# Another order of a step's stages and another set of streamed weight halves, in a four-layer attention kernel on one core

## The chip, the cores and the metric

The kernel runs on one core of one Trainium2 chip. The core has a matrix engine (PE, with its weight loads shown as PEld), a vector engine (DVE), a scalar engine (ACT), a general engine (POOL), and a queue engine (SP) that here only issues transfers; 16 DMA engines move data between the chip's memory (HBM) and the core's own memory. Each engine runs its instructions in its own order and waits on semaphores for the others. The metric is the device time of one execution in microseconds (us); lower is better.

## The reference

Two kinds of layer alternate, A, B, A, B, on a sequence of 2048 tokens of width 640. Each is added to its input after a layer norm.

```python
def _A_ref(x, mem0, Wq, Wk, Wv, Wo, seg_len):     # 32 heads of 192, 8 memory tokens, segments of 32
    for s in range(n_seg):                        # 64 segments, one after the other
        h = jnp.concatenate([mem, xs], axis=1)    # 8 + 32 tokens
        ...                                       # q, k, v; masked softmax; p v
        o = jnp.einsum('bhte,hed->btd', o, Wo)
        mem = o[:, :M, :].copy()                  # the next segment's memory
        outs.append(o[:, M:, :])

def _B_ref(x, wqkv, wo):                          # 32 heads of 20; each token sees itself and
    ...                                           # the 7 tokens at distances 2, 4, ... 14 before it

x = x + _A_ref(_layernorm(x), ...)
x = x + _B_ref(_layernorm(x), ...)
x = x + _A_ref(_layernorm(x), ...)                # the same weights again
x = x + _B_ref(_layernorm(x), ...)
```

The segments of an A layer form a chain, because each takes its memory from the one before. A segment has only 40 rows, while the weights of an A layer are 640 x 6144 four times: every segment needs all of them.

## The kernel before

**A step.** The kernel runs 67 steps (0 to 66), written out in full. Step s works on segment s of the first A layer and segment s - 2 of the second A layer at once: both use the same weights, so their rows stand side by side (`l` = 0 and 1, 2 x 40 columns) in every matmul. The B layers run one step behind, on what the step before left (`xr`). The last step has no A work left, and the first no B work.

**Stages.** A step is a list of named stages, `ORDER` (L58 to L63). `stages()` turns it into a list, and the loop in `run` (L585 to L595) calls one function for each word. For the A layers:

- `q0` to `q15`: queries and keys of two heads, 30 matmuls from two weight halves into one accumulator (`qk_ps`, L323, L328); in all but q0 the first half is read by the first 15 matmuls, the second by the last 15. ACT copies the result to one of five `QK` tiles (L330).
- `s0` to `s3`: scores of four such units (eight heads), 32 small matmuls (L340, L346), then the softmax on DVE and ACT (L350 to L363).
- `t0` to `t3`: transposes of the probabilities (L370), and two masked copies on DVE (L373).
- `va`, `vb`, `vc` 0 to 3: values. `va` and `vb` (`v_seg`) read two weight halves each for the segment's rows (L385). `vc` (`v_mem`) reads the same four halves again for the memory rows (L398). ACT copies both to the tile `V` (L389, L402).
- `pv0` to `pv3`: probabilities times values (L411), copied by ACT to `ot` (L414).
- `o0` to `o14`: output projection, one half of Wo each (o14: two), all into one accumulator (L428).

For the B layers: `ln10` (layer norm sums, L298, L299, then DVE and ACT up to `xnB`, L312), `qkv0` (75 matmuls, L473; three ACT copies, L475; then products on DVE and POOL, L480), `logits0` (L489, softmax up to `attn`, L508), `e0` to `e4` (one matmul each, L515, then a product and a sum on DVE, L518, L520, up to `oT`), `wo0` (L527), `ln20` (the norm for the next step's second A segment) and `store0` (every fourth step). `input0` normalises the next 128 input rows (every fourth step), and `alpha0` is one POOL copy (L287) of the next step's input segment.

**What sets the order.** PE and SP run exactly in the order of the list (`manual_schedule`). DVE, ACT and POOL are ordered by the tile framework's scheduler. All waits are set by the framework: a tile's buffer is given to a new tile when the last reader of the old one is done. PE's results share six accumulator buffers; the output projection has its own.

**Weights.** The four A weights are cut into 64 halves of 128 x 1920 bf16 (480 KB): 0 to 31 are keys and queries (2i and 2i + 1 belong to q_i), 32 to 47 values (four for each of the groups 0 to 3), 48 to 63 the output projection. 32 of them (`RESIDENT`) are loaded once and stay. The other 32 (`STREAMED`, L79) are loaded again in every step into the ring `wt`, which has `RING` = 5 buffers. `half(h)` (L236) issues the load at the place of the stage that reads it first: from the weights in step 0 (with a copy to `Wr`, in the order the ring wants), and after that from `Wr` in two transfers of 240 KB each on SP's queue (L250). SP runs ahead of PE until the ring is full; then it stands until PE is done with a half.

Of the kernel before, what the change touches and what calls it, by code (L numbers as in the profile page):

```python
# [55 lines left out]


ORDER = """  # L58
q0 q1 ln10 alpha0 q2 input0 q3 s0 va0 vb0 vc0 qkv0 q4 t0 q5 q6 q7
s1 pv0 va1 vb1 vc1 logits0 q8 o0 q9 t1 o1 e0 q10 o2 e1 o3 q11  # L60
s2 pv1 va2 vb2 vc2 e2 q12 o4 q13 e3 t2 q14 o5 e4 q15 wo0
s3 pv2 va3 vb3 vc3 o6 o7 ln20 store0 t3 o8 o9 pv3 o10 o11 o12 o13 o14
"""  # L63


# [10 lines left out]
PLAN = stages()  # L76


STREAMED = (1, 5, 6, 7, 8, 11, 13, 14, 15, 17, 22, 23, 25, 26, 29, 30, 31, 33, 35, 38, 41, 46, 48, 49, 50, 51, 53, 55, 56, 58, 60, 63)  # L79
RESIDENT = set(range(N_HALVES)) - set(STREAMED)  # L80
assert len(RESIDENT) == N_RESIDENT

# [570 lines left out]
```

## Time and profile before

| what | value |
|---|---|
| median of three runs | 3643.86 us (3640.27 to 3645.96) |
| the profiled execution's own time | 3648.06 us |
| its span on the core | 3646.3 us |
| mean granted clock of PE | 0.982 of full |
| PE, weight loads busy | 90%, 78% of the span |
| DVE, ACT, POOL busy | 55%, 57%, 10% |
| read from HBM | 1059.73 MB, 296 GB/s over the span |
| first q0 to first q0 of step 1 | 124 us |
| a step between step 4 and step 63 | 53.3 us in the mean (51.6 to 56.6) |

A busy share says how long an engine had work, not whether it held the others up. PE has the most, so what counts is the time in which PE stands; the view of waits lists it by who ended it. The chain of waits follows the end of the run back from each piece of work to what released it. "L328" is a line of the kernel; "wt<-Wr" is the load of a streamed half. [...]

### The profile page before, as it was taken

The page shows a single profiled execution, that of the slowest core. Times are in us where ns is not written, and L with a number is a line of the kernel's source. Part 1 is how long each engine was busy: PE and PEld are TensorE (multiplying, and loading weights), DVE is VectorE, ACT ScalarE, POOL GpSimd, SP SyncE. Part 2 cuts the span into 40 slices and gives each one's busy share as a digit, 9 for nine tenths or more (in the row PEclk, how much of TensorE's full clock was granted, in tenths as well). Part 3 has the DMA queues.
Part 4 walks back from the last instruction along what each step waited for, and adds up shares of the span by engine and source line. Part 5 has one row for each costly group of instructions (what it writes and reads, how often), then busy time and mean ns, then how long its engine had stood idle before and what let it go on. Part 6 is the DMA issues. An engine that isn't in the chain of part 4 may idle for free.

```text
span 3646.3 us, 185054 instructions
## 1 busy us (share of the span) xinstructions
PE 3293.8 (90%) x83325; PEld 2826.4 (78%) x83325; DVE 1994.9 (55%) x5057; ACT 2084.7 (57%) x4533; POOL 378.9 (10%) x467
## 2 busy tenths in 40 slices
PE   5789999999999999999999999999999989999997
PEld 3677787787878777777878777887778777778876
DVE  1346556555555655555565555556555555555554
ACT  2355665565655566565556556565666555655554
POOL 3110010110111001011100101110010110111000
PEclk7799999999999999999999999999999999999998
DMA  9989999898989999999999999999999988999995
GB/s 353 343 283 297 298 301 300 294 304 294 304 291 306 297 302 302 298 304 301 295 302 298 299 299 303 297 307 304 303 302 304 300 288 289 303 299 303 301 301 188
DMA packets 646218, 1090.19 MB, mean 299 GB/s; under 512 B 68648, under 2 KB 642736, under 8 KB 645424
## 3 DMA queue, kind: packets, MB, share of 16 engines
q1 hardware_dynamic: 640560, 1060.00, 88.4%
q8 instruction: 651, 10.67, 1.2%
q0 software_dynamic: 2560, 15.73, 1.1%
q10 hardware_dynamic: 2304, 2.62, 0.2%
q14 instruction: 143, 1.17, 0.1%
HBM read 1059.73 MB, written 18.35 MB: 296 GB/s over the span
## 4 chain that ended last, share of the span: by engine, by line
PE 56%; DMA 16%; DVE 11%; ACT 10%; issue 4%; SPq 3%; POOL 0%; ACTq 0%; POOLq 0%; DVEq 0%
PE qk_ps L328 18%; DMA wt<-Wr 12%; PE v_ps L385 9%; PE acc L428 8%; PE v_ps L398 5%; ACT V L389 3%; PE qkv_ps L473 3%; ACT V L402 3%; ACT QK L330 3%; PE s_ps L346 2%; PE o_ps L411 2%; DVE oT L520 2%; PE qk_ps L323 2%; PE s_ps L340 2%; SPq L250 2%
## 5 line engine op out<-in xcount | busy, mean ns | idle before, releaser
L330 ACT CAST QK<-qk_ps 128x480 bf16<-128x480 f32 x1056 | 578.6, 559 | 949.0 <-PE qk_ps L328 699.0
L328 PE MATMUL qk_ps<-ST,wt 128*128 128x80 bf16 x15840 | 718.8, 203 | 62.6 <-DMA wt<-Wr 45.1
L328 PEld LDWEIGHTS <-wt 128*128 128x128 bf16 x15840 | 628.4, 100 | 96.8 <-DMA wt<-Wr 64.9
L328 PE MATMUL qk_ps<-ST,res 128*128 128x80 bf16 x13860 | 625.4, 203 | 11.6 <-issue 6.0
L328 PEld LDWEIGHTS <-res 128*128 128x128 bf16 x13860 | 562.4, 101 | 39.8 <-issue 10.4
L389 ACT CAST V<-v_ps 64x384 bf16<-64x384 f32 x1056 | 495.8, 469 | 150.5 <-PE v_ps L385 131.4
L428 PE MATMUL acc<-ot,wt 128*128 128x80 bf16 x9900 | 498.4, 202 | 17.6 <-DMA wt<-in_A_Wo_dram 8.5
L402 ACT CAST V<-v_ps 32x384 bf16<-32x384 f32 x1056 | 494.7, 468 | 22.5 <-PE v_ps L398 3.2
L385 PE MATMUL v_ps<-res,ST 128*64 128x384 bf16 x3630 | 488.6, 331 | 13.0 <-DMA res<-in_A_Wv_dram 12.1
L428 PEld LDWEIGHTS <-wt 128*128 128x128 bf16 x9900 | 420.6, 100 | 33.0 <-issue 11.1
L414 ACT CAST ot<-o_ps 128x480 bf16<-128x480 f32 x528 | 269.3, 561 | 221.9 <-PE o_ps L411 220.6
L385 PEld LDWEIGHTS <-ST 128*64 128x64 bf16 x5280 | 286.5, 112 | 132.8 <-issue 26.5
L350 DVE TENSOR_TENSOR sb<-s_ps,maskA 128x320 f32<-128x320 f32 x264 | 129.1, 489 | 444.8 <-PE s_ps L346 444.8
L520 DVE TENSOR_REDUCE oT<-prod 128x64 bf16<-128x512 bf16 x330 | 337.6, 1024 | 8.9
L385 PE MATMUL v_ps<-wt,ST 128*64 128x384 bf16 x1650 | 320.1, 330 | 7.5 <-DMA wt<-in_A_Wv_dram 6.1
L428 PE MATMUL acc<-ot,res 128*128 128x80 bf16 x5940 | 300.6, 203 | 8.9 <-issue 5.6
L480 POOL TENSOR_TENSOR prod<-qT,kh 128x1280 bf16<-128x1280 bf16 x66 | 204.8, 3103 | 742.9 <-ACT kh L475 742.9
L428 PEld LDWEIGHTS <-res 128*128 128x128 bf16 x5940 | 251.4, 100 | 32.1 <-issue 28.1
L518 DVE TENSOR_TENSOR prod<-bc_ps,vh 128x512 bf16<-128x512 f32 x330 | 226.6, 687 | 79.4 <-PE bc_ps L515 79.4
L398 PE MATMUL v_ps<-res,ST 128*32 128x384 bf16 x3630 | 266.3, 331 | 0.0
L398 PE MATMUL v_ps<-wt,ST 128*32 128x384 bf16 x1650 | 264.5, 331 | 0.4 <-issue 0.4
L356 DVE TENSOR_REDUCE sm<-sb 128x8 f32<-128x320 f32 x264 | 128.3, 486 | 166.3 <-ACT sb L354 166.3
(121 smaller groups left out, 3960.7 us busy)
## 6 DMA issues: line engine op xcount, KB each, us to landing
wt<-Wr SPq DMA_DIRECT2D x4160, 240.0 KB, 4.6
Wr<-wt POOLq DMA_DIRECT2D x32, 480.0 KB, 6.6
wt<-in_A_Wq_dram SPq DMA_DIRECT2D x11, 480.0 KB, 9.4
res<-in_A_Wv_dram SPq DMA_DIRECT2D x11, 480.0 KB, 12.1
res<-in_A_Wk_dram SPq DMA_DIRECT2D x10, 480.0 KB, 9.7
wt<-in_A_Wo_dram SPq DMA_DIRECT2D x10, 480.0 KB, 9.7
wt<-in_A_Wk_dram SPq DMA_DIRECT2D x6, 480.0 KB, 8.7
res<-in_A_Wo_dram SPq DMA_DIRECT2D x6, 480.0 KB, 10.7
```

The costliest lines, as they stand in the source:

```text
L328: nc.tensor.matmul(ps[:, m, :, :], lhsT=w[m // 3][:, c, (m % 3) * P:(m % 3 + 1) * P], rhs=st[:, c, PAD:WIDE], start=(c == 0), stop=(c == N ...
L330: nc.scalar.copy(out=self.QK[i % NQK][:, 0:12 * LT].rearrange("p (m l t) -> p m l t", m=6, l=2), in_=ps[:, :, :, :].rearrange("p m t l -> ...
L350: nc.vector.tensor_tensor(out=sb[:, :, :], in0=sv, in1=self.maskA[:, :].unsqueeze(1).to_broadcast([P, 8, LT]), op=ALU.add)
L385: nc.tensor.matmul(ps[r:r + 64, :], lhsT=st[:, c, MID:WIDE], rhs=self.wv[j][:, c, :], start=(c == 0), stop=(c == NCH - 1), tile_position=( ...
L389: nc.scalar.copy(out=self.V[r:r + 64, j, :], in_=ps[r:r + 64, :])
L398: nc.tensor.matmul(ps[r:r + 32, :], lhsT=st[:, c, 0:MID], rhs=self.wv[j][:, c, :], start=(c == 0), stop=(c == NCH - 1), tile_position=(0, ...
L402: nc.scalar.copy(out=self.V[r:r + 32, j, :], in_=ps[r:r + 32, :])
L414: nc.scalar.copy(out=ot[:, :, :, :], in_=ps[:, :, :, :, :].rearrange("p j n l t -> p (j n) l t"))
L428: nc.tensor.matmul(a[:, at, :, :], lhsT=w[h][:, m, dc * P:(dc + 1) * P], rhs=self.ots[h // 2][:, 3 * (h % 2) + m, :, :], start=(h == 0 and ...
L480: eng.tensor_tensor(out=self.prod[:, :, l, :, :], in0=qT[:, :, l, :].unsqueeze(2).to_broadcast([P, NCH, BW, SEG]), in1=window(kh, l), op=A ...
L518: nc.vector.tensor_tensor(out=pv, in0=ps[:, :, :, :], in1=window1(self.vh, c), op=ALU.mult)
L520: nc.vector.tensor_reduce(out=self.oT[:, c, :].rearrange("p (l t) -> p l t", l=2), in_=pv.rearrange("p l w t -> p l t w"), op=ALU.add, axi ...
```

## The change

It writes the list of stages in another order and names another 32 halves as streamed. No stage is added, taken away or changed inside; the number of halves, of transfers and of bytes stays.

```diff
 ORDER = """
-q0 q1 ln10 alpha0 q2 input0 q3 s0 va0 vb0 vc0 qkv0 q4 t0 q5 q6 q7
-s1 pv0 va1 vb1 vc1 logits0 q8 o0 q9 t1 o1 e0 q10 o2 e1 o3 q11
-s2 pv1 va2 vb2 vc2 e2 q12 o4 q13 e3 t2 q14 o5 e4 q15 wo0
-s3 pv2 va3 vb3 vc3 o6 o7 ln20 store0 t3 o8 o9 pv3 o10 o11 o12 o13 o14
+q0 q1 ln10 q2 q3 qkv0 s0 va0 vb0 q4 q5 q6 t0 q7 vc0 logits0 input0 q8 s1 pv0 q9 o0 q10 va1 vb1 vc1
+e0 t1 q11 o1 o2 o3 e1 q12 e2 s2 pv1 va2 vb2 vc2 o4 q13 e3 alpha0 q14 t2 o5 q15 o6 e4 s3 pv2 va3 vb3
+vc3 o7 o8 wo0 t3 o9 o10 o11 pv3 store0 ln20 o12 o13 o14
 """
...
-STREAMED = (1, 5, 6, 7, 8, 11, 13, 14, 15, 17, 22, 23, 25, 26, 29, 30, 31, 33, 35, 38, 41, 46, 48, 49, 50, 51, 53, 55, 56, 58, 60, 63)
+STREAMED = (
+    2, 4, 7, 9, 11, 12, 13, 14, 16, 18, 20, 22, 24, 26, 30, 32, 33, 37, 41, 42, 45, 47, 48, 50, 51, 53, 54, 56,
+    57, 59, 61, 63,
+)
```

By stage, the streamed halves were and are:

| stages | before | after |
|---|---|---|
| q0 to q3 | 1; 5; 6, 7 | 2 (q1); 4 (q2); 7 (q3) |
| group 0 of v | 33 (va), 35 (vb) | 32, 33 (both va) |
| q4 to q7 | 8; 11; 13; 14, 15 | 9; 11; 12, 13; 14 |
| q8 to q11 | 17; -; -; 22, 23 | 16; 18; 20; 22 |
| groups 1, 2, 3 of v | 38; 41; 46 | 37; 41, 42; 45, 47 |
| q12 to q15 | 25; 26; 29; 30, 31 | 24; 26; -; 30 |
| o | 48, 49, 50, 51, 53, 55, 56, 58, 60, 63 | 48, 50, 51, 53, 54, 56, 57, 59, 61, 63 |

## The prediction

> **What bounds the kernel now.** I read, in order: the page's span and busy times, the waits of PE, one step of the chain of waits and of the timeline, the loads' own line, and the granted clock in a few stretches. Of the span 124 us are step 0 (all weights arrive from HBM) and some 30 us the last step, which has no attention; between lie 65 steps of 53.3 us each (step ends read off the timeline). PE is the engine that is never long without work, so a step is the PE work in its written order plus what PE waits for.
>
> ```profile
> span 3646.3 us, 185054 instructions
> PE 3293.8 (90%) x83325; PEld 2826.4 (78%) x83325; DVE 1994.9 (55%) x5057; ACT 2084.7 (57%) x4533; POOL 378.9 (10%) x467
> ```
>
> The waits, over the whole run: who waited <- for whom: us, times, longest.
>
> ```profile
> PEld L340 <- ACT QK L330: 96.1, 197, 0.8
> PEld L515 <- DVE attn L508: 85.8, 66, 3.2
> PEld L328 <- DMA wt<-Wr: 64.9, 134, 2.3
> PE y_ps L527 <- DVE oT L520: 17.4, 34, 1.9
> PE o_ps L411 <- DVE PT L373: 9.4, 42, 0.2
> ```
>
> The first is s0, s1 and s2 standing right behind the last q whose copy they need (197 = 3 x 66: 0.49 us each). The second is e0, too close behind logits0: 1.30 us in each step. The third, 1.0 us a step, is streamed weight halves that come late, mostly the pair 30, 31 at q15.
>
> A step in the chain: start, us, what. It gives the PE prices: one q 1.08, the two halves of a v group 1.64 and its memory rows 0.93, qkv 2.29, a transpose group 0.22.
>
> ```profile
> 1866.37 1.64 PE v_ps L385 x20
> 1868.01 0.93 PE v_ps L398 x20
> 1868.93 2.29 PE qkv_ps L473 x75
> 1871.22 1.08 PE qk_ps L328 x30
> 1872.30 0.22 PE pt_ps L370 x4
> ```
>
> The streamed loads, two per half (ns of an issue: least/median/most), and their landing:
>
> ```profile
> L250 SPq DMA_DIRECT2D wt<-Wr x4160: 319/422/2778, 134.1 to 3609.1; - x199
> ...
> DMA to landing us min/median/max: 2.5/4.6/9.4
> ```
>
> **What the change removes.** s0 gets qkv0 in between, s1 gets vc0, logits0 and q8, s2 gets o1 to o3, e1, q12 and e2: each more than the 0.5 us of the wait, so the 96 us go. e0 moves from 3.4 us of PE work behind logits0 to about 7, more than the 4.75 us that attn took in the step from 1860: 86 us go. wo0 moves from right behind e4, q15 to behind s3, the v group 3 and o8 (over 4 us, two DVE operations of 0.69 and 1.02 us): 17 us. pv3 gets two more o behind t3: 9 us. Sum 209 us. The 65 us of late halves I do not credit: the pair at q15 goes, but places with as little room (va1, o6, o14) come. Next after the softmaxes comes DVE at s3, with e4's work just ahead; by the copies and reductions in the rows t3 has about 5.0 us and needs 4 to 5. I take nothing (up to 0.3 us a step).
>
> **What it adds.** Bytes, packets and issues stay the same: 32 halves a step, on SP's queue in the new order. The ring has five buffers, and a half holds its buffer until its last reader on PE is done. A v half is read by va or vb and again by vc. Now va0, vb0, vc0 stand together; afterwards q4, q5, q6, t0 and q7 lie between vb0 and vc0, and both halves of va0 (32, 33) are streamed. So two of five buffers are shut through four q, which want halves 9, 11, 12, 13, 14.
>
> 1. *q6.* With 32 and 33 held, the load of 13 needs the buffer of 9, free at the end of q4. SP's queue stands there; behind it wait 14, 16 and 18. Half 13 is wanted in the middle of q6, one and a half q later: 1.6 us. It needs 0.2 us to the issue (release to issue in the timeline), 0.4 us to the second issue, and a landing. Bounds 2.5 (least) and 4.6 (median, with others in flight). Nearest are 17 loads in steps 3 to 63 whose forerunner landed within 1.7 us of their first issue: 3.1 to 5.4 us from first issue to second landing, in the middle 4.1, that is 3.6 to 3.7 behind the second issue. I take 3.6: 0.2 + 0.4 + 3.6 = 4.2 us, a wait of 2.6 (1.5 to 3.6). 65 x 2.6 = 169 us. All of PE stands behind it.
> 2. *q7.* 14 needs the buffer of 11, one q later, and now shares the engines with 13: 0.6 + 4.6 = 5.2 us behind q5; q7 comes 3.9 us behind q5 (1.08, the wait of 2.6, 0.22). By the median 1.3, by 3.6 it is 0.3; 0.9 taken: 59 us.
> 3. *q10, va1.* 20 and 37 need the buffers of 32 and 33, free behind vc0; to q10 there are 4.1 us of PE work (logits0, q8, s1, pv0, q9, o0), against 0.6 plus 3.6 to 4.6. 0.1 to 1.1, and up to 0.2 for va1; 0.5 taken: 33 us.
> 4. *qkv0.* It waits for xnB, and its cover of s0 and the v group is gone. From the first ln_ps matmul to the end of xnB are 3.22 us in the timeline (start, us):
>
> ```profile
> 1806.80 0.31 PE L298 MATMUL ln_ps<-xr,ones_b 128*128 128x64 bf16 x5
> ...
> 1809.53 0.49 DVE L312 TENSOR_TENSOR xnB<-xc,ln_r 128x320 bf16<-128x320 f32 x1 [1.08 <-ACT ln_r L256]
> ```
>
> PE has ln10 (0.42), q2 and q3 (2.15) to fill it: 2.57. Wait 0.65 (0.6 if ACT puts the Ln ahead of a QK copy, 1.0 if behind): 42 us. Behind it on PE stand s0 and everything else. Its three ACT copies and the 3.1 us POOL product come earlier, with over 8 us until logits0: nothing (cover gone: 3.1 us less that room, none).
> 5. *o12.* Only ln20 (0.35) instead of o10, o11 lies behind pv3; the copy it reads lands about 0.55 us behind pv3's end. 0.15 taken (0 to 0.3): 10 us.
> 6. *The clock.* PE now has a hole of 2.6 us in each step, and 0.9 us soon after. Before, holes that long are rare, and the granted clock answers them:
>
> ```profile
> 3072.48 0.87 PE L328 MATMUL qk_ps<-ST,wt 128*128 128x80 bf16 x12 [2.18 <-DMA wt<-Wr]
> 243.00:246.40 3.40, 3.40 (x66) 2.54 (x62) 2.23 (x6) 1.61 (x4) 0.45 (x1) 0.50 0.86 301
> 3072.60:3076.00 3.40, 3.40 (x83) 3.27 (x83) 0.95 (x4) 0.56 (x1) 0.45 (x1) 0.51 1.02 382
> 244.59 2.59 PE v_ps L385 x20
> ```
>
> (timeline; busy time by stretch, where PEclk is the third number from the end; chain.) After idle times of 1.92 us at 239.1 and 2.18 us at 3070.3 PE had half the clock for 3.4 us; the v halves took 2.59 instead of 1.64. Holes of 1.25 (e0) mostly did not do it, nor did one of 1.75 us at 1180.9; two drops (649, 823) came behind two or three short holes of 1.1 to 1.6 us together. So a drop costs up to 1.7 us; some of it falls into the waits of q7 and q10. Price 0.9 a step (0 if none, 1.7 if each counts in full): 59 us. [...]
>
> [...]
>
> The rest of what moves. ln20 comes 2.2 us of PE work plus o12's wait before the next q0; its chain behind PE took 2.3 us at the least: margin near nothing, taken as nothing (0 to 0.5 a step; the DVE and ACT queues are empty there). alpha0 (one POOL copy, 0.38 us) comes later in the order; POOL is 10% busy and its wait was for the v rows of the step before: nothing. input0 (10 transposes and DVE copies in 15 steps) now stands ahead of alpha0, whose copy still reads the single buffer of xnt: nothing if the copy goes early as now, up to 3.1 us (the POOL product) in 15 steps, 47 us, if not. Step 0 holds 32 and 33 too, once: 0 to 10 us.
>
> **Sum.** Added 169 + 59 + 33 + 42 + 10 + 59 = 372, removed 209: +163 us. The profiled execution took 3648.06 us (span 3646.3), 4.2 above the median of the three runs. 3648 + 163 = 3811, as a median 3807.
>
> **The rivals.**
> *A. Holes, but full clock.* The drop takes a longer hole, or the wait comes out too short for it: 372 - 59 - 209 = +104, 3748. For it: 1.25 and 1.75 us did nothing. [...]
> *B. Slow landing.* A load behind a shut ring still lands in the median 4.6, and each hole costs a drop in full: 65 x (1.0 for q6, 0.4 for q7, 0.8 for q10 and va1, 0.8 for the clock) = 195 more: 4002 at the worst, 3905 with half of it. Against it: the ring is nearly empty then.
> *C. Faster: a load that goes alone lands quickly, and the clock stays.* With a landing of 2.5 us q6 waits 1.5, q7 0.3, q10 nothing: 65 x (1.5 + 0.3 + 0.65 + 0.15) = 169 against 209, and 35 more for the pair that leaves q15 (0.54 a step): -75, 3569; at 3.0 us -42, 3602. It decides from a landing of some 3.5 us down, where these waits come to the 3.7 us a step that go. For it: 2.5 was seen; against it: the middle of the 17, and the clock.
> *D. It does not do this:* nothing holds the buffers. Excluded as far as the code goes: vc reads the same tiles.
> *E. Gains and waits cancel,* within 0.2% (7 us, about what three runs of this kernel can tell): 0.04.
>
> **Chances.** Forecast 0.40 (its own range 3760 to 3860), A 0.26, B 0.15, C 0.15, E 0.04. Slower 0.81, same 0.04, faster 0.15. The range runs from 3630 (half of C is below) to 3900 (half of B above).
>
> **What would show it.** Right: PE at L328 waits for wt<-Wr some 3.5 us a step, twice in most steps, at q6 and q7; SPq waits there for the q matmuls; the waits for QK and attn fall to near zero; xnB appears as a wait of qkv_ps L473; the clock row shows 0.5 stretches in most steps. Wrong: if half 13 lands within 1.6 us of q4's end, if the hole is under 1.5 us, or if the halves of va0 are late already; and if DVE, with its new order, makes t1, t2 or t3 the next wait.

## The result and the profile after

The changed kernel takes 3829.16 us (median of four runs, 3822.04 to 3848.03) against 3642.07 us for the kernel before (3639.97 to 3645.96): a ratio of 1.052, 95% interval 1.0479 to 1.0562. It is 187 us slower; 163 more were forecast. Its profiled execution took 3848.03 us, the longest of its four, and is 200 us above that of before.

The head of the page after; each engine's busy time, its share of the span, and the instructions:

```profile
span 3846.2 us, 184843 instructions
PE 3431.1 (89%) x83325; PEld 2912.4 (76%) x83325; DVE 2057.7 (54%) x5057; ACT 2115.8 (55%) x4533; POOL 396.3 (10%) x467
```

The same 83325 matmuls keep PE busy for 137 us more than before, so part of the loss is pace. PE's idle time grew by only 63 us, and that is a balance. The waits of PE after (who <- for whom: us, times, longest):

```profile
PEld L330 <- DMA wt<-Wr: 246.6, 274, 2.7
PE qkv_ps L475 <- DVE xnB L314: 34.2, 66, 2.3
PE qk_ps L325 <- DVE ST L441: 31.4, 14, 3.6
PEld L430 <- DMA wt<-Wr: 25.1, 52, 1.8
PE y_ps L529 <- DVE oT L522: 5.3, 5, 1.9
PEld L517 <- DVE attn L510: 3.2, 1, 3.2
```

The waits of s0 to s2 for the QK copies (96.1 us) and of e0 for `attn` (85.8) are gone, but for a single case of the latter. In their place the wait for streamed halves went from 64.9 to 246.6 us, on some four occasions a step. Two rows are new in size: qkv0 for `xnB`, and q0 for `ST`, which the forecast did not have.

SP's queue, which issues the loads, before and after:

```profile
SPq L250 <- PE qk_ps L328: 366.9, 609, 2.2
SPq L250 <- PE v_ps L398: 298.7, 130, 4.8
```

```profile
SPq L252 <- PE qk_ps L330: 594.9, 628, 5.5
SPq L252 <- PE v_ps L400: 383.6, 159, 4.3
```

SP stands 228 us longer for the q matmuls that hold the buffers, up to 5.5 us at once, and 85 us longer for the vc matmuls, the last readers of the v halves.

PE's timeline in one step, from the second half of q5 to q7 (start, duration, the instructions; in brackets the idle time before them and who ended it). The first row is the second half of q5 and the first half of q6:

```profile
1972.74 1.24 PE L330 MATMUL qk_ps<-ST,wt 128*128 128x80 bf16 x30
1975.03 0.28 PE L330 MATMUL qk_ps<-ST,wt 128*128 128x80 bf16 x3 [1.04 <-DMA wt<-Wr]
1975.61 0.60 PE L330 MATMUL qk_ps<-ST,wt 128*128 128x80 bf16 x12 [0.30 <-DMA wt<-Wr]
1976.05 0.39 PE L372 MATMUL pt_ps<-ident,Pm 128*128 128x128 bf16 x4
1977.68 0.28 PE L330 MATMUL qk_ps<-ST,wt 128*128 128x80 bf16 x3 [1.25 <-DMA wt<-Wr]
1978.27 0.98 PE L330 MATMUL qk_ps<-ST,wt 128*128 128x80 bf16 x12 [0.31 <-DMA wt<-Wr]
```

The holes are in the middle of q6 (half 13) and at the head of q7 (half 14). Each is in two pieces, because a half comes in two transfers and three matmuls need only the first. The chain of waits through the second hole shows the mechanism whole: the end of q5 releases SP's queue, the load of half 14 goes out, and q7 goes on when it has landed.

```profile
1971.19 2.27 PE qk_ps L330 x60
1973.46 0.02 issue
1973.47 0.32 SPq L252
1973.79 0.04 issue
1973.84 4.39 DMA wt<-Wr
1978.22 0.04 issue
1978.27 1.98 PE qk_ps L330 x27
```

Half 13 has the same story one q earlier: in each of the steps 4 to 63 its load goes out 0.03 us behind the end of q4.

Busy times by stretch of the profile after (third number from the end: PE's granted clock):

```profile
200.00:3700.00 3500.00, 3185.35 (x78173) 2712.39 (x78170) 1930.92 (x4742) 1983.86 (x4254) 341.51 (x369) 0.96 0.85 283
...
1978.30:1981.70 3.40, 3.40 (x47) 2.53 (x51) 0.00 (x0) 0.56 (x1) 0.00 (x0) 0.50 0.75 254
```

Behind the second hole PE has half the clock (granted 0.50) for 3.4 us, just where vc0 runs: its 20 matmuls take 1.71 us in this step (1980.18 to 1981.89 in the timeline), against 0.93 before. By the granted clock of steps 4 to 63, 56 of the 60 steps have such a stretch (4.66 us a step in the mean), where before 4 had one (0.23 us a step). 55 of the 68 stretches begin at q6, t0 or q7.

The balance of a step, from the traces (mean of steps 4 to 63, us; idle is time in which PE runs no matmul, by who ended it):

| per step | before | after | difference |
|---|---|---|---|
| idle for streamed halves | 0.66 | 3.62 | +2.96 |
| idle for QK copies, `attn`, oT, PT, ot | 2.68 | 0.00 | -2.68 |
| idle for `xnB` at qkv0 | 0.00 | 0.49 | +0.49 |
| idle for ST at q0 | 0.10 | 0.52 | +0.42 |
| other idle time (issue and small ones) | 0.64 | 0.44 | -0.20 |
| busy | 49.27 | 51.46 | +2.19 |
| step | 53.35 | 56.53 | +3.18 |

Nearly all the promised waits went. What came is a wait of about the same size for the weights, most of it close together at q6 and q7, and a slower clock behind it.

### The profile page after: what moved, and what is told of

It is laid out like the page before. It is cut to its first block, busy times and chain, and to the rows that moved or that the text cites. A ratio compares the mean times of both kernels' runs of the same rounds, so it can differ in the third digit from the quotient of the medians.

```text
span 3846.2 us, 184843 instructions
## 1 busy us (share of the span) xinstructions
PE 3431.1 (89%) x83325; PEld 2912.4 (76%) x83325; DVE 2057.7 (54%) x5057; ACT 2115.8 (55%) x4533; POOL 396.3 (10%) x467
## 4 chain that ended last, share of the span: by engine, by line
PE 64%; DMA 25%; DVE 4%; SPq 3%; ACT 2%; issue 2%; POOLq 0%; ACTq 0%; POOL 0%; DVEq 0%
DMA wt<-Wr 21%; PE qk_ps L330 21%; PE v_ps L387 10%; PE acc L430 9%; PE v_ps L400 7%; PE qkv_ps L475 4%; SPq L252 2%; PE s_ps L348 2%; PE o_ps L413 2%; PE s_ps L342 2%; PE qk_ps L325 2%; PE bc_ps L517 2%; DMA x_sb<-in_A_x_dram 1%; PE pt_ps L372 1%; DVE xnB L314 1%
## 5 line engine op out<-in xcount | busy, mean ns | idle before, releaser
L330 PE MATMUL qk_ps<-ST,wt 128*128 128x80 bf16 x14850 | 764.4, 208 | 225.0 <-DMA wt<-Wr 205.5
L330 PEld LDWEIGHTS <-wt 128*128 128x128 bf16 x14850 | 645.1, 104 | 285.4 <-DMA wt<-Wr 246.6
L330 PE MATMUL qk_ps<-ST,res 128*128 128x80 bf16 x14850 | 716.5, 207 | 12.8 <-DMA res<-in_A_Wq_dram 6.5
L330 PEld LDWEIGHTS <-res 128*128 128x128 bf16 x14850 | 626.2, 104 | 43.9 <-issue 23.8
L387 PE MATMUL v_ps<-res,ST 128*64 128x384 bf16 x2970 | 443.6, 330 | 9.1 <-DMA res<-in_A_Wv_dram 7.7
L430 PEld LDWEIGHTS <-wt 128*128 128x128 bf16 x9900 | 418.0, 100 | 36.6 <-DMA wt<-Wr 25.1
L387 PE MATMUL v_ps<-wt,ST 128*64 128x384 bf16 x2310 | 384.2, 330 | 22.3 <-DMA wt<-Wr 12.8
L375 DVE TENSOR_SCALAR PT<-pt_ps,maskL 128x320 bf16<-128x320 bf16 x528 | 182.2, 377 | 283.3 <-PE pt_ps L372 283.3
L430 PEld LDWEIGHTS <-res 128*128 128x128 bf16 x5940 | 261.9, 101 | 52.5 <-issue 44.0
L400 PE MATMUL v_ps<-res,ST 128*32 128x384 bf16 x2970 | 297.8, 356 | 0.1
L400 PE MATMUL v_ps<-wt,ST 128*32 128x384 bf16 x2310 | 296.1, 364 | 0.6 <-issue 0.6
L470 POOL COPY vh<-vh 128x140 bf16<-128x140 bf16 x65 | 19.9, 307 | 2178.7 <-DVE prod L520 2178.7
```

The source lines that it names most:

```text
L330: nc.tensor.matmul(ps[:, m, :, :], lhsT=w[m // 3][:, c, (m % 3) * P:(m % 3 + 1) * P], rhs=st[:, c, PAD:WIDE], start=(c == 0), stop=(c == N ...
L375: nc.vector.tensor_scalar(out=self.PT[g % 2][:, :, :, l, :], in0=ps[:, :, :, 0:LT], scalar1=self.maskL[:, l:l + 1], scalar2=None, op0=ALU. ...
L387: nc.tensor.matmul(ps[r:r + 64, :], lhsT=st[:, c, MID:WIDE], rhs=self.wv[j][:, c, :], start=(c == 0), stop=(c == NCH - 1), tile_position=( ...
L400: nc.tensor.matmul(ps[r:r + 32, :], lhsT=st[:, c, 0:MID], rhs=self.wv[j][:, c, :], start=(c == 0), stop=(c == NCH - 1), tile_position=(0, ...
L430: nc.tensor.matmul(a[:, at, :, :], lhsT=w[h][:, m, dc * P:(dc + 1) * P], rhs=self.ots[h // 2][:, 3 * (h % 2) + m, :, :], start=(h == 0 and ...
```

## The experiments

My theory: in the new order the two halves of va0 hold two of five buffers until vc0, behind q7, so SP's queue stands while q4 to q7 want five halves, and the hole this makes also costs clock. The main rival was that the order itself, or the order of DVE's and ACT's work that it brings, is at fault, and the halves only the place where it shows. Ratios are each to the kernel before in runs on the same chip, with 95% intervals.

**The changed kernel again** (`order_only`). This was meant to be the new order with the old set, but the edit left the set as it was. So the expectation below is not tested by it, and the run only repeats the changed kernel.

> The new order with the old set of streamed halves. Shut-ring theory (v halves of group 0 keep their buffers until vc0, behind q7): the old set has one streamed half in va0 (33) and one in vb0 (35), so the ring is shut by two buffers here as well; half 14 then has its buffer only from the middle of q4 and 15 from the end of q5, and by 4.2 us a load q7 waits 2.5 to 3 us in two pieces, o3 (51 behind 22, 23, 49 and 50) about 1.5: some 4.5 us of late halves a step, clock drops in most steps, 3800 to 3860 us. Rival, the set is at fault (32 and 33 both in va0, 12 and 13 both in q6): the late halves go and what is left is the gain of the order, 209 us less 42 for qkv0: 3460 to 3560.

Measured: 3823.54 us, 1.0527 (1.0491 to 1.0563), step 56.09 us. The result repeats. It ran together with the next three and serves as their standard.

**The old order with the new set** (`set_only`).

```diff
-q0 q1 ln10 q2 q3 qkv0 s0 va0 vb0 q4 q5 q6 t0 q7 vc0 logits0 ...
+q0 q1 ln10 alpha0 q2 input0 q3 s0 va0 vb0 vc0 qkv0 q4 t0 q5 q6 q7
+(and the other three lines of before)
```

> The old order with the new set. Shut-ring theory: va0, vb0, vc0 stand together, so nothing is shut through q4 to q7 and the waits at q6 and q7 are under 0.3 us a step; o11, o13 and o14 are thin (their buffers come free at vc3 and o6): 1.2 to 2 us of late halves a step against 1.0 before, waits for QK and attn as before, few clock drops: 3670 to 3760 us. Rival, the set is at fault: q6 and q7 wait 2.5 to 3.5 us as in the changed kernel, and with the old waits for QK and attn back the time is 3950 to 4050.

Measured: 3770.86 us, 1.0388 (1.035 to 1.0425). Its waits:

```profile
PEld L343 <- ACT QK L333: 96.9, 198, 0.8
PEld L431 <- DMA wt<-Wr: 94.1, 177, 2.1
PEld L518 <- DVE attn L511: 74.9, 61, 3.3
PEld L331 <- DMA wt<-Wr: 53.8, 110, 1.8
PE y_ps L530 <- DVE oT L523: 51.0, 70, 1.9
```

The old waits are back, as they must be. The idle time is 0.23 us a step at q7 and under 0.1 at q6: with vc0 right behind vb0, and then qkv0, which reads no streamed half, the load of 13 is on time and that of 14 nearly so. The new halves are late elsewhere instead, at o13, o14 and va0 above all (2.0 us a step over all stages, 0.66 before), and wo0's wait for oT, the last row, is 0.70 us a step against 0.19. So this set is poor for the old order too, a little more than expected. Neither half of the change is good alone with the other half's old partner, as the next run shows.

**The new order with the old set** (`order_old_set`).

```diff
-STREAMED = (2, 4, 7, 9, 11, 12, 13, 14, ..., 32, 33, ...)
+STREAMED = (1, 5, 6, 7, 8, 11, 13, 14, 15, ..., 33, 35, ...)
```

> The new order with the old set of streamed halves. Shut-ring theory: 33 (va0) and 35 (vb0) keep two buffers until vc0 here as well; 14 gets its buffer in the middle of q4 and 15 at the end of q5, so q7 waits 2.5 to 3 us in two pieces, and o3 (51) about 1.5 us: 3.5 to 4.5 us of late halves a step, clock drops in most steps, time 3800 to 3860 us, as the changed kernel. Rival, the set is at fault: late halves at 1 us a step as before, and the 209 us of the order less 42 for qkv0 are won: 3460 to 3560.

Measured: 3851.33 us, 1.0575 (1.0532 to 1.0617). Its waits:

```profile
PEld L327 <- DMA wt<-Wr: 244.7, 312, 3.2
PEld L427 <- DMA wt<-Wr: 62.7, 110, 2.1
PE acc L427 <- ACT ot L413: 20.6, 9, 3.7
```

The old set too streams two halves of group 0 (33 and 35), so two buffers are shut through q4 to q7 here as well. The hole moves to q7 (2.13 us of idle time a step), where 14 and 15 are wanted, and others open at q12 and o3. SP issues half 15 only at the end of q5, in each of the steps 4 to 63. So another set with two halves of group 0 has the same wait, one q later. In every fourth step o12 now also stands some 2.5 us, 0.58 us a step in the mean; 0.34 of it is put down to the copy of pv3's result, the third row (more on it at the third set).

**vc0 back behind vb0, all else as changed** (`vc0_back`).

```diff
-... qkv0 s0 va0 vb0 q4 q5 q6 t0 q7 vc0 logits0 input0 q8 ...
+... qkv0 s0 va0 vb0 vc0 q4 q5 q6 t0 q7 logits0 input0 q8 ...
```

> The changed kernel with one word moved: vc0 right behind vb0. Shut-ring theory: 32 and 33 give their buffers to 13 and 14 at the end of vc0, 2.7 us ahead of the middle of q6, instead of 1.6 us: q6 waits about 1.5 us, q7 0.2, fewer clock drops; 1.6 us a step less of waits and 0.5 to 1.5 less of the clock: 3640 to 3710 us. Rival, four q with five streamed halves in a row are too dense whatever the ring holds: both waits stay at 3.4 us and the time at 3810 to 3840.

Measured: 3725.93 us, 1.0257 (1.0217 to 1.0297): 98 us under the repeat, by one word moved. The idle time for halves falls from 3.51 to 2.35 us a step, at q6 from 1.98 to 0.65, and the half-clock stretches from 4.27 to 1.82 us a step. It is less than I expected, because q7 still waits 1.29 us. SP's queue shows why:

```profile
SPq L252 <- PE v_ps L400: 656.0, 195, 6.8
```

In the repeat this row has 379.3 us and 158 cases: SP stands longer for the vc matmuls here, not shorter. The halves of va0 are still held until vc0 ends. In each of the steps 4 to 63 the load of 13 goes out there, and that of 14 right behind it, 0.9 us after vc0's end in the middle of them. From its first issue to its second landing half 14 then takes 4.95 us in the middle of these steps (4.33 to 5.77 for eight tenths), while between vc0 and q7 PE has only q4, q5, q6 and t0, some 3.5 us of work. In the old order the 2.29 us of qkv0 lie in between; here qkv0 comes earlier. So this run lets the two buffers go earlier, but not early enough. It gives back about half of the loss of 191 us on that chip; whether the rest comes of the same buffers, or of five streamed halves wanted in four q, it can't tell. The third set below can.

**Dummy work in the holes** (`fill_hole`). The waits stay, but PE is kept at work in them: 55 matmuls ahead of half 13 at q6 and 20 ahead of half 14 at q7, whose product the true matmuls overwrite. It prices the clock.

```diff
+                for _ in range({(6, 3): 55, (7, 0): 20}.get((i, m), 0) if self.step else 0):
+                    nc.tensor.matmul(ps[:, m, :, :], lhsT=self.wqkv[:, 0, 0:P], rhs=st[:, 0, PAD:WIDE], start=True, stop=True)
```

> The changed kernel, and PE is kept busy in the two holes: 55 matmuls of 128x80 (2.0 us) ahead of the second half of q6 and 20 (0.7 us) ahead of q7, on weights that are there, written where the true product is then begun afresh. The halves land no earlier. Clock theory (a hole of 2.4 us brings half clock for 3.4 us, which costs 1 to 1.7 us of work): no 0.5 stretches in most steps, the granted clock back at 0.98, time 70 to 120 us less: 3710 to 3760. Rival, the drops fall into waits and cost nothing: same time, 3815 to 3845, at most some 10 us more where the filling outlasts the hole.

Measured: 3790.18 us, 1.0436 (1.0403 to 1.0468): 33 us under the repeat, well under what I expected. Page head and waits:

```profile
span 3783.8 us, 194593 instructions
PE 3496.3 (92%) x88200; PEld 3013.7 (80%) x88200; DVE 2056.7 (54%) x5057; ACT 2112.2 (56%) x4533; POOL 397.4 (11%) x467
```

```profile
PE qk_ps L332 <- DMA wt<-Wr: 80.8, 155, 2.5
PE qkv_ps L477 <- DVE xnB L314: 31.2, 63, 2.3
PE qk_ps L325 <- DVE ST L443: 29.6, 14, 3.2
PE v_ps L389 <- DMA wt<-Wr: 20.1, 28, 1.6
```

The half-clock stretches fall from 4.27 to 0.85 us a step. Without the dummies' time, a step's busy time falls by 1.25 us (51.20 in the repeat, 49.95 here), but its idle time, the dummies' counted in, grows by 0.67 (4.89 to 5.56). From the start of one stage to the start of the next, what is gained between t0 and q8 is in part lost again at o0, q10, va1 and o14 (0.08, 0.30, 0.13 and 0.10 us a step): a faster PE reaches the next late half earlier, and waits there for what it has gained. So about half of the clock's gross price was not a price. The dummies also cost something themselves. Where the landing is on record, they end after the half's second transfer in 23 of 52 steps at q6 and in 17 of 53 at q7; by how late the true matmul then starts I estimate 0.2 us a step, some 15 us in all. The 33 us are a lower bound.

**The input rows a step earlier** (`early_x`) **and in mid-step** (`mid_x`). The new row, q0 waiting 31.4 us for `ST`, has 14 cases: every fourth step, when 128 new input rows (`x_sb`) are loaded on SP's queue at the head of the step. DVE stands at their statistics (`bst`), in its own order ahead of the last copy into `ST`:

```profile
DVE bst L271 <- DMA x_sb<-in_A_x_dram: 64.2, 16, 12.0
```

Before, the same row had 24.7 us. In the trace after, q0 starts 2.8 us behind the landing of `x_sb` in each such step.

```diff
-                if s % 4 == 1 and 4 * (s // 4 + 1) < self.n_seg:
+                if s % 4 == 0 and 4 * (s // 4 + 1) < self.n_seg:
```

> The changed kernel with the load of the next 128 input rows (x_sb) issued a step earlier. In the changed kernel's trace the first q0 in every fourth step starts 2.8 us behind the landing of x_sb, since DVE stands at the statistics of these rows with the copies for q0 behind them. Theory, x_sb is what q0 waits for: PE's wait for ST at q0 falls from 0.5 to under 0.15 us a step, 20 to 30 us less, 3795 to 3810. Rival, it is ln20, which stands closer to the end now: the wait stays and the time too (3820 to 3835).

Measured: 3828.91 us, 1.0516 (1.0487 to 1.0545): no gain.

```profile
PE qk_ps L325 <- DVE ST L441: 28.7, 14, 2.9
```

The wait stays, and moves with the load from the steps 1, 5, 9 ... to the steps 0, 4, 8 .... DVE's order follows the load: the scheduler puts the statistics at the next step's head as soon as the load comes a step earlier. The cause is supported, the remedy was wrong. Next the load went out ahead of q7, away from any step's head:

```diff
-                if s % 4 == 1 and 4 * (s // 4 + 1) < self.n_seg:
-                    self.input_load(s // 4 + 1)
+                    if (what, i) == ("q", 7) and s % 4 == 1 and 4 * (s // 4 + 1) < self.n_seg:
+                        self.input_load(s // 4 + 1)
```

> The changed kernel with the load of the next 128 input rows placed ahead of q7, in the middle of the step instead of at its start. With the load a step earlier PE's wait at q0 only went from every step behind a multiple of four to the step before. Theory, DVE stands at the rows' statistics wherever the load lands near a step's end: q0's wait for ST falls from 0.5 to under 0.1 us a step, 20 to 33 us less than the changed kernel (3795 to 3810), unless DVE's stand then holds s1's softmax. Rival: q0 keeps its wait, same time.

Measured: 3798.85 us, 1.0456 (1.0413 to 1.0498). The waits for halves are as in the changed kernel, and no row of q0 for `ST` is left:

```profile
PE qk_ps L330 <- DMA wt<-Wr: 214.3, 250, 2.2
PE qkv_ps L475 <- DVE xnB L314: 32.6, 64, 2.3
```

By the ratios this is some 23 us less than the changed kernel (1.0456 against 1.052; their intervals meet), most of the 31.4 us of the row that went.

**The changed order with a third set** (`order_other_set`). The order is left as changed; of group 0 no half is streamed, so nothing is held from va0 to vc0.

```diff
-STREAMED = (2, 4, 7, 9, 11, 12, 13, 14, 16, 18, 20, 22, 24, 26, 30, 32, 33, 37, 41, 42, 45, 47, 48, ...)
+STREAMED = (0, 3, 4, 5, 7, 8, 9, 11, 13, 14, 16, 18, 20, 21, 22, 24, 25, 27, 29, 31, 39, 42, 45, 48, 50, 52, 54, 55, 56, 57, 59, 60)
```

> The changed kernel's order with a third set of streamed halves, in which no half of v group 0 is streamed and q4 to q7 stream five halves (8, 9, 11, 13, 14), chosen by adding up when each buffer comes free, 4.2 us a load. Shut-ring theory: nothing is shut between vb0 and vc0, late halves fall from 3.6 to 1 or 1.5 us a step, the clock drops go, and the order's gain (QK, attn, oT, PT) shows: 3530 to 3620 us. Rival, the order is slow in itself (five streamed halves in four q behind each other, or DVE and ACT in the new order): q6 and q7 still wait 2 us or more, 3720 to 3830.

Measured: 3551.62 us, 0.9775 (0.9749 to 0.98). The changed order is faster than before by 2.3% (2.0 to 2.5 by the interval), with the same number of halves and bytes, only others.

```profile
PE qk_ps L327 <- DMA wt<-Wr: 47.4, 123, 2.3
PE acc L427 <- ACT ot L413: 26.6, 13, 2.6
...
PE qkv_ps L472 <- DVE xnB L311: 12.3, 24, 2.3
```

The idle time for halves is 0.87 us a step (3.62 in the changed kernel), and the half-clock stretches 0.68 us (4.66). The rival falls: the order isn't at fault. Between this run and the changed kernel lie some 270 us by the ratios, and they hang on nothing but which 32 halves are streamed. The number of halves wanted close together isn't it: q4 to q7 stream five here as well, and all the stages up to q7 ten in both kernels. What differs is when a buffer comes free for them. Half 13 goes out 6.9 us ahead of q4's end (the middle of steps 4 to 63; 0.03 us behind it in the changed kernel), and neither 13 nor 14 is late in any of these steps. This also answers what `vc0_back` left open: with no half of group 0 in the ring both waits go.

q0's wait for `ST` is gone here too, but it has only moved. In every fourth step o12 waits some 2 us for a copy of pv3's result, the second row above. ACT has the norm of the new input rows (`lnst`) ahead of that copy, in its own order, and `lnst` waits for DVE's statistics, which wait for the rows to land:

```profile
1178.92 0.89 DVE L268 BATCH_NORM_STATS2 bst<-x_sb 128x6 f32<-128x320 bf16 x2 [1.97 <-DMA x_sb<-in_A_x_dram]
1180.09 0.29 ACT L254 ACTIVATE lnst<-lnst,eps 128x1 f32<-128x1 f32 x1 [3.69 <-DVE lnst L269]
1180.41 1.02 ACT L413 CAST ot<-o_ps 128x480 bf16<-128x480 f32 x2
1181.02 0.69 PE L427 MATMUL acc<-ot,wt 128*128 128x80 bf16 x8 [2.52 <-ACT ot L413]
```

**Small moves in the order of before** (`small_moves`, `small_moves_set`). If the gains that the prediction named are real (the waits for QK, `attn` and oT), they should be had without parting vc0 from vb0. `small_moves` keeps the old set and moves single stages, and the input load a step earlier; `small_moves_set` is the same with a set chosen for it.

```diff
-q0 q1 ln10 alpha0 q2 input0 q3 s0 va0 vb0 vc0 qkv0 q4 t0 q5 q6 q7
-s1 pv0 va1 vb1 vc1 logits0 q8 o0 q9 t1 o1 e0 q10 o2 e1 o3 q11
-s2 pv1 va2 vb2 vc2 e2 q12 o4 q13 e3 t2 q14 o5 e4 q15 wo0
-s3 pv2 va3 vb3 vc3 o6 o7 ln20 store0 t3 o8 o9 pv3 o10 ...
+q0 q1 ln10 alpha0 q2 input0 q3 va0 s0 vb0 vc0 qkv0 q4 t0 q5 q6 q7
+pv0 s1 va1 vb1 vc1 logits0 q8 o0 q9 t1 o1 q10 e0 o2 o3 e1 q11
+pv1 s2 va2 vb2 vc2 e2 q12 o4 q13 e3 t2 q14 o5 e4 q15
+pv2 s3 wo0 va3 vb3 vc3 o6 o7 t3 ln20 store0 o8 o9 pv3 o10 ...
...
-STREAMED = (1, 5, 6, 7, 8, 11, 13, 14, 15, 17, ...)
+STREAMED = (1, 2, 5, 7, 8, 9, 10, 14, 15, 16, 17, 18, 21, 22, 23, 24, 25, 26, 29, 30, 31, 34, 35, 38, 41, 45, 46, 49, 55, 56, 60, 61)
```

(The last line is in `small_moves_set` alone.)

> The kernel before with its own set and small moves that leave each v group together: va0 ahead of s0, pv0 ahead of s1, pv1 ahead of s2, pv2 ahead of s3 and wo0 behind it, e0 behind q10, e1 behind o3, t3 ahead of ln20, and x_sb a step earlier. Theory (the order's gains are real, only the shut ring ate them): waits for QK from 1.15 to 0.2 us a step, for attn from 1.1 to 0.3, late halves up by 0.5 to 1 us as PE comes sooner: 60 to 100 us less than before, 3540 to 3590. Rival (PE's waits only move to the next late thing, halves or DVE): within 20 us of before.

> The same moves and another set, chosen by adding up for each half when its buffer comes free, 4.2 us a load and 1.2 us between landings. Theory: late halves at 1 to 1.5 us a step instead of 2: 3500 to 3560 us. Rival: the adding up misses the spread of the landings, and the set is no better than the old one (3550 to 3600) or worse.

Measured: 3557.85 us, 0.9771 (0.9743 to 0.9799), and 3533.68 us, 0.9701 (0.9663 to 0.974), the lowest ratio of all runs. The waits of the second:

```profile
PEld L328 <- DMA wt<-Wr: 99.0, 179, 2.0
...
PE qk_ps L323 <- DVE ST L439: 13.5, 14, 1.9
```

The rows for QK and `attn` have gone here too, for little in return: the step is 51.37 us, and 1.17 us of it is idle time for halves (0.66 before), most of it at q11 and q15.

**The same with the input load ahead of q7** (`small_moves_set_mid_x`; the edit is that of `mid_x`).

> The small moves with their set, and the input rows loaded ahead of q7. Theory: q0's wait of 0.3 us a step goes, 10 to 20 us less than with the load at the step's start: ratio to before 0.964 to 0.968. Rival: the time is set by late halves at q11 and q15, which then take up what is won: 0.970.

Measured: 3542.46 us, 0.9755 (0.9725 to 0.9786): no gain. q0's wait for `ST` goes, but t0 now waits 0.34 us a step for DVE's `Pm` and pv0 0.20 for `PT`. Both waits stand in the same steps, every fourth, so here too DVE's work on the new rows seems only to fall on another reader.

A ring of six buffers would have tested the shut buffers most directly. It was not run.

## Why the prediction was right, point by point

The direction, the mechanism and the size came as forecast: +187 us by the medians, +163 forecast. In a step that is 3.18 us against 2.5. That the size came so close is in part luck: the waits at q6, q7, q10 and va1 were put 0.9 us a step too high (4.0 against 3.1), the clock 1.3 too low, the waits that go 0.5 too high, and one wait of 0.42 was missed.

1. *q6.* 2.6 us forecast; 2.09 of idle time measured. The term behind it, the landing of half 13, was forecast at 4.0 us from first issue to second landing (0.4 + 3.6), and is 4.09 in the middle of steps 4 to 63 (3.15 to 4.79 for eight tenths of them). Two readings behind it were off and nearly cancel: the issue follows the release by 0.03 us, not 0.2, and of the 17 loads that served as the nearest case the one in the middle took 4.2 us from first issue to second landing, 3.85 behind the second issue, where 4.1 and 3.6 to 3.7 were read. Counted with the three matmuls that need only the first transfer and run inside it, the hole is 2.37 us.
2. *q7.* 0.9 forecast, 0.81 measured. In `vc0_back` it is 1.29, since there half 14 goes out right behind 13 and both wait for vc0; with nothing of group 0 in the ring it is gone (`order_other_set`).
3. *q10, va1.* 0.5 forecast, 0.20 measured, but 0.58 where the clock is held (`fill_hole`: 0.33 and 0.25). The working for a PE at full clock was right; at half clock PE comes later to both.
4. *qkv0.* 0.65 forecast, 0.49 measured.
5. *o12.* 0.15 forecast; nothing stands there with this set, though with the two other sets in this order o12 does wait for the copy (0.34 and 0.44 us a step), for a reason that the forecast did not have, the new input rows. Late halves at o14, q12 and vb3 cost 0.46 in its place, which the prediction covered in not crediting the 0.66 a step of late halves that went.
6. *The clock.* The term's two parts were off in opposite ways. That holes of some 2 us would lower the clock in most steps was right (56 of 60). The gross price, 2.19 us a step of longer busy time, is above the 0.9 taken, and even above the 1.7 given as its upper end, because some of the stretches (14 of the 68) last 6.8 us instead of 3.4. The net price is lower: 33 us in `fill_hole`, which left 0.85 of 4.27 us of slow clock in place and lost some 15 us to its own dummies, so it is a lower bound; 59 were forecast. The prediction said that some of it would fall into the waits at q7 and q10. About half did, at q10, va1, o0 and o14; q7 shows no part of it.

Late halves and the clock together were forecast at 4.9 us a step (2.6 + 0.9 + 0.5 + 0.9), with no credit for the 0.66 that went; they came to 2.96 + 2.19 = 5.15.

What was missed lies elsewhere. *The removed waits* were summed to 209 us, 3.2 a step, from the view of all waits, whose rows for the QK copies and `attn` are those of the weight loads (PEld). The matmuls behind them stood for less: 76.1 and 77.1 us in PE's own rows, since PE was still at the end of earlier work while the weight load waited (at 1822.6 in the timeline of before, at s0, the weight load waits 0.51 us and its matmul 0.41). By idle time 2.68 us a step went, so the gain was over-priced by some 0.5. *q0's wait for ST* (+0.42) was in no term. The prediction followed the DVE work of the norm, of the softmaxes and of the products, but not the one DVE instruction that waits for a transfer, though its row was in the trace of before. Less the 0.2 us of "issue" and the like that went, these two make the difference of 0.7 between 2.5 and 3.18. *Step 0* went from 124.3 to 127.9 us, within the 0 to 10 taken. ln20, alpha0 and input0 cost nothing that a row shows.

The rivals: *A* (holes, full clock) would have given 3748 and falls with the clock row; what `fill_hole` gives, 3790, is above it by the waits that grow and by what the sum missed or priced too high. *B* (slow landing) and *C* (quick landing and full clock) were put in landings behind the second issue, and half 13's is 3.7 by that (4.09 less 0.4): well under B's 4.6, and above the 3.5 from which C would have decided, though not by much. C falls on the clock as well.

## What to carry to other kernels

In a ring of streamed weights a tile that has a late second reader closes a buffer for all the work in between, so order and set must be judged together: the same order is 5% slower with one set and 2% faster with another. Before moving a stage, list for each load which reader frees the buffer that it needs, and compare the work from there to its own reader with the landing time in the trace. Price a wait that is to go by the matmul's own row, not by that of its weight load (76.1 against 96.1 us for the QK copies here), and a lower clock by what is late behind it: where the next load is the limit, much of the pace that is lost would have been waited away (in `fill_hole` 1.25 us a step of busy time went and 0.67 of idle time came).

## What the runs showed of the hardware that was not expected

- Idle time of some 2 us a step, in pieces, was enough for half clock in nearly every step: 56 of 60 steps, with 2.09 us of idle time at q6 and 0.81 at q7 in the mean, in pieces of 0.3 to 1.3 us like those in the timeline above. No single long hole was needed. Of the 68 slow stretches 54 last 3.4 us and 14 last 6.8. In the 3.4 us ahead of each of them PE was idle for 1.57 us or more in all, 2.13 in the middle; the longest single piece was 1.5 us in the middle. The sum alone doesn't tell where a slow stretch comes: at 600.7 and 3216.3 us, with 2.2 us idle in the 3.4 us before, none followed.
- In spite of that the clock's net cost is small here: at least 33 us (of 191) for 3.4 us a step of slow clock taken away.
